# Products with a zero operand in a two-layer decode kernel, and new orders of the engines' work

## The chip, the cores and the metric

The kernel runs on one core of a Trainium2 chip. The core has a matrix engine (TensorE, PE in the profile, with its weight loads as PEld), three vector-like engines (VectorE or DVE, ScalarE or ACT, GpSimd or POOL), a queue engine (SyncE or SP) that here only issues DMAs, and sixteen DMA engines between HBM and the on-chip memory SBUF. Matrix products are written to PSUM, eight banks of 128 partitions by 512 fp32 columns. Each engine works through its own list of instructions in order and waits on semaphores for the others. The metric is the time on the device in microseconds (us): the median of several executions, less is better.

## The reference

Eight tokens (one per sequence of the batch, D = 448) go through two layers, which use the same weights and the same caches. Each layer is an attention block and an MLP block, with a residual around each:

```python
W = min(4096, max(256, Sk // 4))            # 1024 of 4096 cached positions
q = x @ wq                                   # 16 heads of 256
k, v = last W positions of the caches        # 8 heads, each used by two of q's
p = softmax(q . k * Dh ** -0.5); o = p . v
A(x) = o @ wo
B(x) = silu(x @ w1) @ w2                     # F = 1792

x = x + A(layernorm(x)); x = x + B(layernorm(x))
x = x + A(layernorm(x)); x = x + B(layernorm(x))
```

Everything is bf16 in memory. The window of the caches is 64 tiles of K and 64 of V (8 rows of the batch by 8 heads), 512 KB each, 67 MB; the weights are about 10.5 MB.

## The kernel before

**Rows.** The kernel goes through the batch row by row (b = 0 to 7). The K and V tiles of a row (sixteen, 8.4 MB) are loaded once and serve both layers, so all of a row's work of layer 1 and its attention of layer 2 happens while they are on the chip. A tile lies in one of 30 slots. The loads are issued by SP in one fixed sequence (K of row 0, `wo`, `w2`, V of row 0, `w1`, K of row 1, and so on), and the load that reuses a slot waits until the last reader of the tile in it is done: K loads of row b+2 wait for layer-2 scores of row b, V loads mostly for its layer-2 values.

**Steps of a row**, by the names that the program gives them:

- `KT`: DVE transposes each K tile in two halves (L629).
- `qbd1` (POOL, L619) spreads the queries of layer 1; `S0` (PE, L644) are the layer-1 scores, in two halves `S0.0`, `S0.1` of four groups of eight products each; `max0`, `mT0`, `mg0`, `mb0` (DVE, L657 to L661) find the maxima; `exp0` (ACT, L663); `perm0` (PE, L665) and `turn0` (DVE, L667) bring the weights p into columns; `l0` sums them.
- `PVA`, `PVD` (PE, L708, L727): values of heads 0 to 3 and 4 to 7. `oevA`, `oevD` (ACT, L697, L702) copy them out, `oTA`, `oTD` (PE, L688) turn them, `oTevA`, `oTevD` (DVE, L682) scale them.
- `woA`, `woD` (PE, L780), `rowb1` (ACT copy, L1054), `fold1` (PE, L498 and L500): output projection, added to x in bank 7.
- The chain between the attentions: `xb1` (DVE, L806), `stat1` (PE, L813), `var1` and `pow1` (the layernorm's scale, ACT L816 and POOL L818), `w1` (PE, L515), `yT` (DVE, L535), `tanh` (ACT, L825), `hT` (DVE, L826), `w2` (PE, L837), `rowb2` (ACT, L841), `fold2`, `xb2`, `stat2`, `var2`, `pow2`, and the queries of layer 2: `wq0`, `wq1` (PE, L864), `qT`, `qm` (DVE, L873), `qd` (PE, L877), `qbd2` (ACT, L881).
- `S1.0`, `S1.1`, `max1`, `exp1`, `perm1`, `turn1`, `l1`, `lc1` (ACT copy of the sums, L673): scores of layer 2, in bank 1 (`SC[1]`). `PV1.0`, `PV1.1` (PE): its values; `oev1`, `oT1`, `oTc1` (ACT, L679) store them for the end.

The layer-1 attention of row b+1 runs beside the chain and the layer-2 attention of row b. The output projection and MLP of layer 2 are done once for rows 0 to 6 (`final_rows`, names ending in 8, row 6.5) during the last row, and then for row 7 (`final_last`, names ending in L).

`stat1` and `oT1` share a bank, and so do other steps; two accesses to one bank from different engines are ordered by semaphores. The start-up work of row 0 also includes sums over the weights' rows (`rsum`, L434 on DVE and L442 on ACT, then `rsumd`), which the projections need for the layernorm's mean.

**What sets the order.** The program adds steps as tasks, one after the other, with the tiles that they read and write. Four strings (`ORDER`) then say for each engine in which order its tasks are emitted: each character is the place, in the list of tasks still left, of the one that comes next. Waits follow from the tiles, whatever the order. Where the text says that a step stands ahead of another, this order is meant. For a row from the middle of the program PE's order before is:

```text
fold1/4 oT1/3 stat1/4 w1/4 S0.0/5 S0.0/5 w2/4 S0.0/5 fold2/4 S0.0/5 wq0/4 stat2/4 wq1/4 qd0/4
S1.0/4 x4  S0.1/5 x4  qd1/4  S1.1/4 x4  perm0/5 l0/5  PVA/5 x4  perm1/4 ...
```

(name/row; x4 are four groups of products).

Of the kernel before, what the change touches and what calls it, by code (L numbers as in the profile page):

```python
# [14 lines left out]

ORDER = {
    "pe": (
        "0000000111110000022222102220100000077066000001111777700000223333200099227011440302200000706605100011"
        "1177770000022333320009222055510020111000070666010001111777700000244440220092222504444100110000706050"
        "0001111177770000024444012009222204440020111000077060510001111777700000223333011092222044410201110000"  # L20
        "70660510001111777700000223333011092222044441001110000777001400cc0bb0000000002233330110bb209110055020"
        "222000009991070550002010333333331011d00000222201000000000"),
    "dve": (
        "CnEDDoo.18B.17AiE.13y2xmd2odEUUErbixAlOzpyA1qNLyttwwhhBrh7yge0dakv0jo2nkici908gf4e4dn772kaaaa4h94215"
        "89940736350dccc03aaaa3321eb0c09b0088700555504000100a90888807700daa0bc0807700555504000000a90888077700"
        "da09a0a087700555504000000a90888077700da0bb00a77700555550000000a90888077700daa0aa0a08700555504000000a"
        "09888078700daa0990a07700555504000000a0898807870b0aba09aa90000555504000000b0ja0088e8d9998000504440300"
        "100001111100000000"),
    "act": (
        "1333342344233413d3c342322252222221111113122222010000000020111111110000002011111100000000201111111000"  # L30
        "00002011100000000000201111111100000020111100000004030200010010000000"),
    "pool": (
        "00010011022002200220022002200320001000"),
}


# [164 lines left out]
def bass_interleave_layers__sliding_block_cached__dense_activation_silu__decode_kernel(  # L201
# [3 lines left out]
    _, HKV, SK, DH = A_k_cache.shape  # L205
# [5 lines left out]
    P = 128  # L211
# [24 lines left out]
    ident = sb("ident", [P, P], BF16)  # L236
# [12 lines left out]
    cols = sb("cols", [P, 10], BF16)  # L249
# [51 lines left out]
    def pe(fns, reads, writes, row, name):  # L301
        add("pe", fns, reads=reads, writes=writes, row=row, name=name)
# [518 lines left out]
    def up(b, name):  # L821
# [4 lines left out]
        dve(lambda e: e.scalar_tensor_tensor(out=hTr[b], in0=th, scalar=1.0, in1=y, op0=ALU.add, op1=ALU.mult),  # L826
            bk(XB) + ["th"], ["hT"], b, "hT" + name)

    def chain(b):
        xcols(b, "1")  # L830
        stats(b, "1")
        up(b, "")
        if b < LAST:
            fns = []
            for f in range(FC):
# [3 lines left out]
                    stop=(f >= FC - 4), tile_position=(0, 32 * (f % 4)), skip_group_check=True))  # L839
# [3 lines left out]
        else:  # L843
            WB = (XB, LB[1])
            for part in range(2):
                fns = []
                for f in range(FC):
# [3 lines left out]
                        start=(f < 4), stop=(f >= FC - 4), tile_position=(0, 32 * (f % 4)), skip_group_check=True))  # L851
# [10 lines left out]
        for k2 in range(2):  # L862
# [4 lines left out]
                start=(c == 0 and s == 0), stop=(c == KC - 1 and s == 1), tile_position=(0, 32 * j), skip_group_check=True)  # L867
# [101 lines left out]
    def final_last(s):  # L969
        b = LAST  # L970
        scr = slots[s][:, :]
        KEY = SL(s)
        xr = scr[:, 0:XC + 1]
        orow = scr[:, 128:128 + 112]
        xrow_f = scr[:, 512:512 + 224].bitcast(F32)
        xs = view(bank[YB][:], 0, [(XS, XC + 1)])
        pe(lambda e: e.matmul(xs, ident[:], x2b[b], start=True, stop=True),
           ["ident", ("x2b", b)], bk(YB), b, "xinitL")
        for i0 in range(0, NCH, 16):
            wo_rows(b, range(i0, i0 + 16), lambda i: oT2[b][:, i % 2, i // 2:i // 2 + 1],  # L980
                    [("oT2", b, i0 // 16)], "woL")
        act(lambda e: e.activation(rowb, bank[XB][:, 0:D + 2], ACTF.Copy), bk(XB), [("rowb", 0), ("rowb", 1)], b, "rowbL")
        fold(b, ["rowb_e", ("rowb", 0), ("rowb", 1)], "L")
        xcols(b, "L")
        act(lambda e: e.activation(xr, bank[YB][:, 0:(XC + 1) * XS:XS], ACTF.Copy), bk(YB), ["xr"] + KEY, b, "xr")
        stats(b, "L")
        up(b, "L")
        ob = bank[OB[0]]
        T = 112
        fns = []  # L990
        for t in range(4):
            for c in range(KC):
                d0, d1 = max(T * t, P * c), min(T * t + T, P * c + P, D)
# [14 lines left out]
        pe(fns, ["hT"] + W2_R, bk(OB[0]), b, "w2L")  # L1008
        dve(lambda e: e.scalar_tensor_tensor(out=orow, in0=ob[:, 0:T], scalar=rhalf, in1=xrow_f, op0=ALU.mult,
                                             op1=ALU.add), bk(OB[0]) + KEY + ["xrowf", "rhalf"], ["orowL"], b, "orowL")  # L1010
        src = bass.AP(orow.tensor, orow.offset, [[32 * orow.ap[0][0], 4], [1, T]])
        dma(lambda e: e.dma_start(out2[b:b + 1].rearrange("o (t n) -> (o t) n", t=4), src), ["out_last"], "out",
            reads=["orowL"])
# [107 lines left out]
```

## Time and profile before

| | us |
|---|---|
| median of 3 runs | 245.74 |
| lowest, highest | 244.15, 248.39 |
| the profiled execution | 246.33 |
| its span, first to last instruction | 244.3 |
| PE busy | 166.2 (68%) |
| DVE busy | 154.6 (63%) |
| ACT busy | 69.5 (28%) |
| POOL busy | 22.8 (9%) |
| mean granted TensorE clock | 0.964 |

The page is of one execution. Its slices divide the span into 40 parts of 6.1 us; a digit is the busy share in tenths. PEclk is the share of full speed that the clock of TensorE was granted. "Chain" is the work that ended last, followed back from the end: what each step waited for. Rows of groups give the line of the code, the engine, the tiles and their shapes, how many there were, the time that they were busy and the mean time of one in ns, then idle time of the engine just ahead of them and what ended it. The span leaves out what lies around the program: 246.33 against 244.3.

### The profile page before, as it was taken

The page shows a single profiled execution, that of the slowest core. Times are in us where ns is not written, and L with a number is a line of the kernel's source. Part 1 is how long each engine was busy: PE and PEld are TensorE (multiplying, and loading weights), DVE is VectorE, ACT ScalarE, POOL GpSimd, SP SyncE. Part 2 cuts the span into 40 slices and gives each one's busy share as a digit, 9 for nine tenths or more (in the row PEclk, how much of TensorE's full clock was granted, in tenths as well). Part 3 has the DMA queues.
Part 4 walks back from the last instruction along what each step waited for, and adds up shares of the span by engine and source line. Part 5 has one row for each costly group of instructions (what it writes and reads, how often), then busy time and mean ns, then how long its engine had stood idle before and what let it go on. Part 6 is the DMA issues. An engine that isn't in the chain of part 4 may idle for free.

```text
span 244.3 us, 7993 instructions
## 1 busy us (share of the span) xinstructions
PE 166.2 (68%) x3521; PEld 93.1 (38%) x3521; DVE 154.6 (63%) x412; ACT 69.5 (28%) x205; POOL 22.8 (9%) x42
## 2 busy tenths in 40 slices
PE   0000516376879587978787887779779787998872
PEld 0000503023553345445444434443454444356532
DVE  2019897999774685668477758945864983165501
ACT  2000004991223522331332223233223322233230
POOL 1000030002001100100011002001000200011100
PEclk9999999999999899979999999999999998599996
DMA  6999999999989997999999999989999998000000
GB/s 158 401 406 404 380 380 406 407 408 411 404 294 372 415 406 253 388 413 373 331 412 409 379 385 412 408 298 406 412 365 369 413 406 302 3 3 3 3 4 1
DMA packets 23400, 78.18 MB, mean 320 GB/s; under 512 B 3127, under 2 KB 6086, under 8 KB 22982
## 3 DMA queue, kind: packets, MB, share of 16 engines
q1 hardware_dynamic: 22806, 77.30, 81.8%
q8 instruction: 27, 0.44, 0.7%
q10 hardware_dynamic: 560, 0.38, 0.7%
q14 instruction: 7, 0.06, 0.1%
HBM read 77.67 MB, written 0.01 MB: 318 GB/s over the span
## 4 chain that ended last, share of the span: by engine, by line
PE 42%; DVE 25%; DMA 14%; ACT 8%; issue 5%; SPq 3%; POOL 2%; DVEq 0%; ACTq 0%
DMA slot<-in_A_k_cache_dram 14%; PE bank L644 11%; DVE slot L629 9%; PE bank L708 6%; PE bank L780 5%; PE bank L864 5%; PE bank L837 3%; DVE slot L434 3%; SPq L455 2%; PE bank L877 2%; PE bank L727 2%; PE bank L515 2%; ACT rowb L841 2%; PE bank L498 2%; DVE bank L535 1%
## 5 line engine op out<-in xcount | busy, mean ns | idle before, releaser
L629 DVE STREAM_TRANSPOSE slot<-slot 128x512 uint32<-128x512 uint32 x128 | 82.3, 683 | 17.4 <-DMA slot<-in_A_k_cache_dram 17.2
L644 PE MATMUL bank<-slot,qbd 128*16 128x256 bf16 (+1 forms) x1024 | 40.7, 292 | 10.9 <-ACT qbd L881 5.2
L708 PE MATMUL bank<-slot,qbd 128*4 128x512 bf16 (+1 forms) x384 | 29.4, 406 | 7.5 <-DVE qbd L667 4.0
L644 PEld LDWEIGHTS bank<-slot,qbd 128*16 128x16 bf16 (+1 forms) x1024 | 25.3, 90 | 21.2 <-ACT qbd L881 7.5
L818 POOL TENSOR_TENSOR fcols<-fcols 128x1 f32<-128x1 f32 x17 | 9.5, 557 | 110.3 <-ACT fcols L816 107.8
L780 PE MATMUL bank<-wo_sb,q1s 128*1 128x449 bf16 x284 | 18.1, 386 | 1.6 <-DVE q1s L682 1.0
L864 PE MATMUL bank<-wq_sb,xbz 128*2 128x256 bf16 x512 | 17.0, 275 | 0.9 <-DVE xbz L806 0.7
L619 POOL TENSOR_TENSOR qbd<-q1s,fcols 128x256 bf16<-128x256 bf16 x16 | 9.5, 612 | 73.9 <-PE bank L688 70.3
L657 DVE TENSOR_REDUCE mm<-bank 128x1 f32<-128x256 f32 x16 | 6.8, 422 | 13.6 <-PE bank L644 13.6
L881 ACT ACTIVATE qbd<-bank 128x256 bf16<-128x256 f32 x16 | 6.1, 383 | 30.6 <-PE bank L877 30.6
L708 PEld LDWEIGHTS bank<-slot,qbd 128*4 128x4 bf16 (+1 forms) x384 | 7.9, 85 | 15.9 <-issue 5.8
L667 DVE STREAM_TRANSPOSE qbd<-bank 128x256 bf16<-128x256 bf16 x16 | 7.4, 463 | 10.1 <-PE bank L772 5.1
L548 PE MATMUL bank<-xb,cols 128*128 128x8 bf16 x4 | 0.3, 174 | 19.9 <-DVE slot L546 19.9
L535 DVE STREAM_TRANSPOSE bank<-bank 128x256 f32<-128x256 f32 (+1 forms) x25 | 10.9, 434 | 4.4 <-PE bank L515 1.5
L663 ACT ACTIVATE qbd<-bank,mm 128x256 bf16<-128x256 f32 x16 | 7.6, 472 | 18.6 <-DVE mm L661 13.8
L864 PEld LDWEIGHTS bank<-wq_sb,xbz 128*2 128x2 bf16 x512 | 11.2, 82 | 4.0 <-DVE xbz L806 1.7
L682 DVE TENSOR_TENSOR q1s<-bank,q1s 128x16 bf16<-128x16 f32 (+1 forms) x18 | 3.0, 168 | 14.2 <-PE bank L688 14.1
L702 ACT ACTIVATE qbd<-bank 128x512 bf16<-128x512 f32 x14 | 8.3, 595 | 10.2 <-PE bank L688 5.7
L697 ACT ACTIVATE qbd<-bank 128x256 bf16<-128x256 f32 x22 | 8.3, 382 | 9.5 <-PE bank L708 3.2
L806 DVE SCALAR_TENSOR_TENSOR xbz<-bank,fcols 128x5 bf16<-128x5 f32 x17 | 3.9, 227 | 10.7 <-PE bank L500 9.4
L727 PE MATMUL bank<-slot,qbd 128*12 128x512 bf16 (+3 forms) x124 | 10.4, 434 | 0.1
L837 PE MATMUL bank<-w_sb,q1s 128*1 128x449 bf16 x98 | 8.3, 434 | 3.1 <-DVE q1s L826 2.9
(156 smaller groups left out, 220.9 us busy)
## 6 DMA issues: line engine op xcount, KB each, us to landing
slot<-in_A_k_cache_dram SPq DMA_DIRECT2D x64, 512.0 KB, 8.5
slot<-in_A_v_cache_dram SPq DMA_DIRECT2D x64, 512.0 KB, 10.5
wo_sb<-in_A_wo_dram SPq DMA_DIRECT2D x1, 3584.0 KB, 25.9
wq_sb<-in_A_wq_dram SPq DMA_DIRECT2D x3, 1024.0 KB, 9.1
w_sb<-in_B_w_dram SPq DMA_DIRECT2D x1, 1568.0 KB, 28.1
w_sb<-in_B_w_dram SPq DMA_DIRECT2D x1, 1344.0 KB, 17.8
wq_sb<-in_A_wq_dram SPq DMA_DIRECT2D x1, 256.0 KB, 3.6
wq_sb<-in_A_wq_dram ACTq DMA_DIRECT2D x1, 256.0 KB, 4.4
```

Of the source, the lines that this page charges most:

```text
L535: dve(lambda e: e.transpose(view(bank[bi][:], n, [(2, n // 32), (n // 16, 16), (1, 2)]), bank[bi][:, 0:n].rearrange("p (g r s) -> p g r s" ...
L619: pool(lambda e, k2=k2: e.tensor_tensor(qdata(0, k2), q1s[:, b, 64 * k2:64 * k2 + 64].rearrange("p (n r) -> p n r", r=2).unsqueeze(3) .bro ...
L629: dve(lambda e, v=v: e.transpose(v, v), SL(s, h), SL(s, h), b, "KT%d" % k)
L644: fns.append(lambda e, w=w, j=j, kv=kv, cb=cb, par=par: e.matmul(sc[32 * j:32 * j + up_to, 0:256], w, kv, start=(cb == 0 and par == 0), st ...
L697: act(lambda e, s=s: e.activation(E_sb[L], ob[:, s * DH:(s + 1) * DH], ACTF.Copy), bk(OB[L]), QB(L, 1), b, "oev%s.%d" % (name, s))
L702: act(lambda e: e.activation(full, ob[:, :], ACTF.Copy), bk(OB[L]), QB(L, 0) + QB(L, 1), b, "oev" + name)
L708: return [lambda e, u=u: e.matmul(bank[OB[L] if ob is None else ob][32 * j:32 * j + 2 * n, :], pT_sb[L][:, pcol(u, c0):pcol(u, c0) + 2 * n ...
L727: pe([lambda e, t=t, c0=c0, w=w, kvh=kvh: e.matmul(bank[OB[0]][32 * t:32 * t + 2 * w, :], pT_sb[0][:, pcol(2 * t, c0):pcol(2 * t, c0) + 2 ...
L780: fns.append(lambda e, i=i, w=w, c0=c0: e.matmul(bank[XB][32 * (i % 4):32 * (i % 4) + 1, c0:c0 + D + 1], oT(i), w, start=(i < 4), stop=(i ...
L818: pool(lambda e: e.tensor_tensor(rhalf, var4, nhalf, ALU.pow), ["var4", "nhalf"], ["rhalf"], b, "pow" + name)
L837: fns.append(lambda e, f=f, w=w, c0=c0: e.matmul(bank[XB][32 * (f % 4):32 * (f % 4) + 1, c0:c0 + D + 1], hTr[b][:, f:f + 1], w, start=(f < 4),
L864: pe([lambda e, j=j, c=c, s=s, wb=wb, k2=k2: e.matmul(bank[wb][32 * j:32 * j + 2, 0:256], pair(b, xcol(c, k2), s), view(wq_sb[:], c * HD + ...
```

## The change

A function `busy(b, n)` adds n tasks on PE. Each is one product of a column of zeros, taken as 128 equal weight columns, with the identity read four times over (512 columns). Its result, zeros, goes over the whole of bank 1, which holds the layer-2 scores later in the row. As it writes that bank, it waits for the bank's readers in the row before. `chain` calls it with 8 in row 0 and 5 in the others, `final_last` with 5: 50 products in all.

All four order strings are new. Read out, PE's order for the row above becomes:

```text
fold1/4 oT1/3 zero/4 stat1/4 w1/4 zero/4 zero/4 zero/4 w2/4 S0.0/5 S0.0/5 fold2/4 S0.0/5 stat2/4 wq0/4 wq1/4
qd0/4 zero/4 S0.0/5  S1.0/4 x4  S0.1/5 x4  qd1/4  S1.1/4 x2  perm0/5  S1.1/4 x2  PVA/5 x4  l0/5 oTA.0/5 ...
```

In the other middle rows the last zero product stands behind `fold2` and the first mostly ahead of `oT1`. On DVE `turn0` moves ahead of `max1`, both halves of a K tile's transposes mostly follow each other, and one half stands between `yT` and `hT`; `oTevD` of rows 1, 2 and 4 moves ahead of the next row's transposes. On ACT `oevA.0` moves ahead of `exp1`, `lc1` ahead of `rowb1` (that of row 5 behind it), and a load of the activation table (the task `init` of L327) moves from row 1, between `oev1` and `oTc1`, to row 5, between `lc1` and `rowb1`. On POOL one of the two `qbd1` moves behind `pow2` from row 4 on. In the start-up many of DVE's small tasks move ahead of the first K tile, and the sums over weights stand elsewhere.

```diff
@@ ORDER
-    "pe": (
-        "0000000111110000022222102220100000077066000001111777700000223333200099227011440302200000706605100011"
...
+    "pe": (
+        "000000011111l111133312223022051002010033300710500300111117777000440033333210011004403330201101044000"
...
@@ up
+    def busy(b, n, row=None):
+
+        for _ in range(n):
+            pe(lambda e: e.matmul(bank[SC[1]][:, :], cols[:, 3:4].broadcast_to([P, P]), view(ident[:], 0, [(0, 4), (1, P)]),
+                                  start=True, stop=True), ["cols0", "ident"], bk(SC[1]), b, "zero")
+
     def chain(b):
+        busy(b, 8 if b == 0 else 5)
         xcols(b, "1")
         stats(b, "1")
         up(b, "")
@@ final_last
         dve(lambda e: e.scalar_tensor_tensor(out=orow, in0=ob[:, 0:T], scalar=rhalf, in1=xrow_f, op0=ALU.mult,
                                              op1=ALU.add), bk(OB[0]) + KEY + ["xrowf", "rhalf"], ["orowL"], b, "orowL")
+        busy(b, 5)
         src = bass.AP(orow.tensor, orow.offset, [[32 * orow.ap[0][0], 4], [1, T]])
```

More of the change, by code (lines that the diff above doesn't have):

```diff
@@ L17 @@
     "pe": (
-        "0000000111110000022222102220100000077066000001111777700000223333200099227011440302200000706605100011"
[L19 to L22, printed above, removed]
@@ L23 @@
-    "dve": (
[L24 to L28, printed above, removed]
+        "000000011111l111133312223022051002010033300710500300111117777000440033333210011004403330201101044000"
@@ new lines @@
+        "1770000300111117777000400444423010011155510022011101044000177005000011111777700040044442320001115514"
+        "0022201101044000177710000011111777700040044442320001161514002201110004400017716111101111177770004004"
+        "4442320001161510022201110105400017771000001111177770004004444232000116151002201111010033001777710100"
+        "ccc0b1111060000444442200011817771002022220000033ccc43a02060500001140333333300110000022220b1200000000"
+        "11000"),
+    "dve": (
+        "pSG0G0bGq0njnwvZtutFtUEg4CQz0g4yBydzjhvHwbvnFrEAAzkayz352iuj9k6q935nikb8g14f2a4439nj90888c8685c09664"
+        "4551122baaa2a929216bd1aaa10077700555555000010098880870705ac09a90087700555550000100098880870705ac09aa"
+        "0077700555550000100a08880878060aab09a0087700555550000100098880870705aa0aa90077700555550000100a088808"
+        "78060aab0990087700555550000100098880778060acb0b99a900005555500000000099ag90ebb8ba8006004403020100001"
+        "111100000000"),
@@ L29 @@
     "act": (
-        "1333342344233413d3c342322252222221111113122222010000000020111111110000002011111100000000201111111000"
-        "00002011100000000000201111111100000020111100000004030200010010000000"),
+        "13333442444455f5e56432322224222111111113312211111111111331211111111111133122111111111113312211111111"
+        "11133122100000000000220111000000000302011000000004002200010010000000"),
     "pool": (
-        "00010011022002200220022002200320001000"),
+        "00010011022002200200020002000010001000"),
```

## The prediction

> **What bounds the kernel now.** I read the page first: its slices, then its chain.
>
> ```profile
> PEclk9999999999999899979999999999999998599996
> DMA  6999999999989997999999999989999998000000
> GB/s 158 401 406 404 380 380 406 407 408 411 404 294 372 415 406 253 388 413 373 331 412 409 379 385 412 408 298 406 412 365 369 413 406 302 3 3 3 3 4 1
> PE 42%; DVE 25%; DMA 14%; ACT 8%; issue 5%; SPq 3%; POOL 2%; DVEq 0%; ACTq 0%
> DMA packets 23400, 78.18 MB, mean 320 GB/s; under 512 B 3127, under 2 KB 6086, under 8 KB 22982
> ```
>
> The DMA row says "always busy" for 34 slices (up to about 207 us), then nothing for 37 us. But the rate row has holes (294, 253, 331, 298, 365). At the 410 GB/s of the good slices 78.18 MB take 191 us; with some 4 us of start the stream could end near 195. So about 11 us are lost in holes, and the chain is mostly PE and DVE: the loads wait for slots that the compute frees late. The DMA queue's own waits agree.
>
> ```profile
> SPq L455 <- PE bank L644: 66.4, 7, 12.2
> ```
>
> The queue that issues K and V loads waits seven times for the score products (L644): a row's layer-2 scores free the slots of the row after next. So the time from one row to the next is compute, and the stream follows. I cut the trace by stretches at the starts of `rowb1` (L1054), once per row:
>
> ```profile
> 80.02:103.19 23.17, 17.93 (x380) 10.24 (x382) 15.24 (x38) 7.46 (x19) 2.21 (x4) 0.93 0.95 362
> 103.19:126.00 22.81, 18.76 (x396) 10.54 (x388) 15.55 (x39) 6.29 (x19) 2.37 (x5) 0.93 0.97 379
> 126.00:147.81 21.81, 17.16 (x388) 9.55 (x382) 15.13 (x37) 6.06 (x18) 2.21 (x4) 1.00 1.01 395
> 147.81:169.31 21.50, 17.40 (x392) 9.56 (x387) 14.60 (x37) 6.36 (x19) 2.37 (x5) 1.00 0.98 377
> 169.31:190.71 21.40, 17.54 (x391) 9.85 (x387) 15.16 (x38) 6.21 (x17) 2.29 (x4) 1.00 0.99 386
> 190.71:215.33 24.62, 20.35 (x400) 10.64 (x396) 14.32 (x38) 6.53 (x21) 1.10 (x2) 0.86 0.66 256
> ```
>
> Columns are the stretch, its length, then busy us of PE, weight loads, DVE, ACT, POOL, then clock, DMA share, GB/s. Rows with clock 1.00 take 21.4 to 21.8 us; the three with a lower clock take 22.8, 23.2 and 24.6. No engine is full (PE 17 to 18 of 21.5 us): a row is a string of waits between engines. The clock itself, stretch by stretch (PE alone):
>
> ```profile
> 83.30:86.70 3.40, 2.71 (x50) 0.50 1.05 414
> 107.20:110.60 3.40, 3.22 (x45) 0.50 1.03 406
> 206.10:213.00 6.90, 6.67 (x61) 0.51 0.18 67
> 240.30:244.30 4.00, 0.61 (x32) 0.50 0.01 2
> ```
>
> Half clock in four stretches, each a multiple of 3.4 us. The stretch of 3.4 us before each fall, and one before which nothing fell:
>
> ```profile
> 79.86:83.27 3.41, 1.26 (x37) 0.96 (x36) 2.94 (x6) 2.85 (x6) 0.00 (x0) 1.00 1.02 417
> 103.75:107.16 3.41, 2.14 (x59) 1.33 (x55) 2.67 (x7) 1.40 (x5) 0.55 (x1) 1.00 1.03 417
> 202.74:206.15 3.41, 1.66 (x42) 1.11 (x31) 0.87 (x3) 0.45 (x2) 0.00 (x0) 1.00 0.75 263
> 236.87:240.28 3.41, 1.99 (x90) 1.71 (x94) 0.83 (x3) 0.86 (x4) 0.55 (x1) 1.00 0.00 0
> 172.01:175.43 3.42, 2.23 (x57) 1.04 (x46) 3.00 (x7) 0.91 (x2) 0.41 (x1) 1.00 1.03 411
> ```
>
> PE was busy 37%, 63%, 49% and 58% of the stretch before a fall, and 65% of one that had none. The line lies near 64%: one product more in a stretch can decide.
>
> **The change part by part.** *The products.* Reading the new PE order out: in rows 1 to 6 mostly one zero product after `fold1`, three between `w1` and `w2`, one after `fold2`; eight in row 0; in the last row five in the chain and five in the final part: 50 in all. Whole-array products of 512 columns have no row in this trace; the nearest are these.
>
> ```profile
> 143.68 1.04 PE L727 MATMUL bank<-slot,qbd 128*16 128x512 bf16 x16
> 149.75 0.24 PE L813 MATMUL bank<-xbz 128*128 128x1 bf16 x4 [0.38 <-DVE slot L629]
> 149.92 0.95 PE L515 MATMUL bank<-w_sb,xbz 128*2 128x224 bf16 x32
> 152.00 0.92 PE L837 MATMUL bank<-w_sb,q1s 128*1 128x449 bf16 x14 [0.50 <-DVE q1s L826]
> 173.46 0.17 DVE L826 SCALAR_TENSOR_TENSOR q1s<-th,bank 128x14 bf16<-128x14 f32 x1 [0.42 <-ACT th L825]
> ```
>
> Sixteen 512-column products, four side by side, take 1.04 us: 0.26 us per set of 512 columns, which I take (from nothing, where it fills a wait, to the double at half clock). So 50 cost 13 us of PE time. But `w1` ends at 150.87 and `w2` starts at 152.00: 1.13 us of waiting for DVE, ACT, DVE, in which three products (0.78 us) fit. Ahead of `stat1` PE idles 0.38 us, so one fits; behind `fold2` I take the same. Today score products of the next row (L644) fill the `w1` gap; the new order moves them behind `w2`, where PE waits for ACT's copy `rowb2`, and behind `qd0`, where it waits for ACT. Cost: 0. A product also waits for readers of its bank; the last, `lc1` on ACT, is moved ahead of `rowb1` in nearly all rows, so it is done by then. If that cover is gone, the 13 us appear.
>
> *What the products give.* In the chain, the same stages at half and full clock:
>
> ```profile
> 70.47 7.13 DMA slot<-in_A_k_cache_dram
> 77.62 1.30 DVE slot L629 x2
> 81.08 1.28 ACT L327
> 82.95 1.29 PE bank L515 x32
> 85.34 1.49 PE bank L837 x8
> 107.38 1.50 PE bank L837 x10
> 119.44 1.06 PE bank L708 x16
> 149.99 0.91 PE bank L515 x21
> 152.00 0.86 PE bank L837 x12
> 203.78 1.15 issue
> 206.20 1.91 PE bank L708 x13
> ```
>
> Row 1: `w1` 1.29 against 0.91, `w2` 1.49 against 0.86: −1.0. Row 2: 0.64 in `w2`, some more in the scores behind it; −1.0 agrees with its 22.81 against 21.6. Last row: the first product of values takes 1.91 where 1.06 is usual (−0.85); the 6.67 us of PE work at half clock would be 3.3 less at full; not all of it is on the path, so −2.8. The fall at 240.3 comes after a 3.4 us stretch whose late part alone gets two products: 0. Together −4.8; bounds 0 and −6.3 (half of 2.71, 3.22 and 6.67).
>
> *The issue gap.* At 203.78 PE stood 1.15 us inside one group of scores with no cause shown, and this made the third fall. Other code lies there now, but such a gap can come elsewhere: −0.6, between 0 and −1.15.
>
> *ACT's table load.* It is moved from row 1, where it holds 1.28 us of the chain between `oev1` and `oTc1` (which `stat1` waits for), to row 5 ahead of `rowb1`.
>
> ```profile
> 167.00 0.18 ACT L673 ACTIVATE q1s<-bank 128x16 f32<-128x16 f32 x1
> 169.31 0.55 ACT L1054 ACTIVATE rowb<-bank 128x450 bf16<-128x450 f32 x1 [2.13 <-PE bank L780]
> ```
>
> There ACT idles 2.13 us, and 1.28 fits. `stat1` waits for `oTc1` without the load too (0.38 us in row 4, above), so 1.28 less 0.38: −0.9, between 0 and −1.28.
>
> *DVE in row 1.* `oTevD` stood behind two K transposes of row 2, which waited for the 7.13 us load above; it now stands ahead of them. But `xb1` still stands behind four. Between 0 and the 1.30 us of the two; I take −0.4.
>
> *Steady rows.* `perm0` moves into the middle of `S1.1`, and `turn0` ahead of `max1`; the exponential it needs is ready no sooner than today, so nothing. Half a K tile's transpose (0.65 us, half of the 1.30) now stands between `yT` and `hT`; DVE idles 0.42 there today, so +0.2 a row. `stat2` moves ahead of `wq0`, so that its power is ready earlier; I take 0.2 a row back for it. Sum 0, bounds ±0.3 in six rows, ±1.8.
>
> *Start.* This row sum of three weight chunks stands on the chain ahead of `turn0` of row 0:
>
> ```profile
> 43.25 2.80 DVE slot L434
> ```
>
> In its place comes one of two chunks, two thirds or 1.9 us by the same row; but two long sums now stand ahead of `max0`, and one more sum on ACT ahead of `exp0`. Half of the 0.9 arrives, −0.5; the bounds are half a sum either way, ±1.5.
>
> **Sum:** −4.8 −0.6 −0.9 −0.4 +0 −0.5 = −7.2. The profiled execution took 246.33 us, 2.03 around a span of 244.3; it lies 0.59 above the median of 245.74. So 246.33 − 7.2 = **239.1 us**, a span of 237.1.
>
> **The rivals.** *The products do not hold the clock*, or the new order opens other gaps: then −0.6, −0.9, −0.4, −0.5 stay: 243.9. For it: with zero weights nothing shows that the gate counts such products as work; one near-miss stretch per row at 65% leaves little margin. Against it: the fall went with PE's busy share in four of four. [...]
>
> *The stream swallows the early rows.* K loads land 7 us or more behind the scores that free their slots, and `xb1` stands behind four transposes of them; if that loop sets the pace, the 3.3 us of rows 1 and 2 (1.0 + 1.0 + 0.9 + 0.4) do not reach the end, nor does the start, and −2.8 and −0.6 stay: 242.9. For it: 70.47 on the chain. Against: 11 us of holes that shrink when slots come free earlier.
>
> *The products stand on the path.* Mechanism: PE works in order, so a product that starts just before its successor is ready holds it, and scores no longer in the `w1` gap lengthen what follows. All 50 exposed with no clock gained: 243.9 + 13 = 256.9; it is over 2% slower from about half exposed (6.8 of 13 us). For it: gaps of 0.3 to 0.4 us hold a 0.26 us product barely. Against: the 1.13 us gap takes three of five.
>
> *More.* With slots free earlier the holes close too: half of 11 us beside the last row's −2.8 and −0.6, and the rest: 246.33 − 5.5 − 3.4 − 1.8 = 235.6.
>
> **How the numbers follow.** Forecast 0.48; clock not held 0.21; stream swallows 0.12; on the path 0.12; more 0.07. Two per cent, about what a measurement of this kernel can tell from no change, are 240.8 and 250.7. Of the forecast's cases most lie under 240.8 (0.43 of 0.48), with *more* 0.50. The path rival gives slower 0.11 (a little of it stays within). The rest, 0.39, is within. Range: from 234.5, past *more*, to 249.0, past 243.9 with the unknowns of start and steady rows added (1.5 + 1.8) and a few products exposed.
>
> **What would show it.** Right: clock 1.00 in all stretches from row 1 to the last scores; row lengths of 21.4 to 21.8 throughout; no table load on the chain; `w1` 0.91 and `w2` 0.86 in rows 1 and 2; the zero products' PE time in stretches that were idle; `rowb1` of the last row near 208 instead of 215.33. Wrong: half-clock stretches as before; `w2` later than 1.15 us after `w1`; `stat1` waiting for the zero products; a gap in ACT's row 5 over 1.3 us; longer holes in the GB/s row.

## The result, and the profile after

The changed kernel takes 235.64 us (median of 4 runs, 235.11 to 237.31) beside 244.94 us for the kernel before (4 runs, 242.53 to 248.39): a ratio of 0.966, with a 95% interval of 0.957 to 0.976. Ratios here leave out runs more than 1.5% above the fastest of their kernel, in each later session more than half of those of the kernel before, so they can show less of a gain than the medians. The forecast of 239.1 us had the sign right, the main mechanism, and two thirds of the gain. The profiled execution took 235.61 us with a span of 233.7, against 246.33 and 244.3.

From the page of the kernel after: granted clock, DMA engines and rate in 40 slices of 5.8 us, then the DMA totals, the queue that brings instructions, the chain's shares, and the group of the zero products.

```profile
PEclk9999999999999999999999999999999999999999
DMA  6999999999999999999999999999999998300000
GB/s 163 413 403 407 379 381 399 407 407 412 405 403 392 414 404 356 365 414 409 400 406 406 400 400 409 409 326 407 410 406 382 411 409 329 127 3 3 3 1 4
DMA packets 23401, 78.20 MB, mean 335 GB/s; under 512 B 3127, under 2 KB 6086, under 8 KB 22982
q8 instruction: 28, 0.46, 0.8%
PE 47%; DVE 22%; DMA 13%; ACT 10%; issue 5%; SPq 2%; ACTq 0%; DVEq 0%
L833 PE MATMUL bank<-ident,cols 128*128 128x512 bf16 x48 | 16.2, 391 | 0.0
```

No slice behind the first record of the clock (at 54.1 us) is under full clock any more, and the holes in the rate row are fewer and shallower: 356, 365, 326 and 329 where there were 294, 253, 331 and 298. PE's share of the chain rose from 42% to 47%, DVE's fell from 25% to 22%. The zero products are 48 (8 in row 0, 5 in each of the seven other rows, 5 at the end), not the 50 that the description and the prediction count. They take 16.2 us, but PE as a whole is busy only 2.0 us longer than before (168.2 against 166.2). The same cut by rows as in the prediction, from one `rowb1` (now L1063) to the next, after; the columns are the stretch, its length, busy us of PE, weight loads, DVE, ACT and POOL, the clock, the DMA share and GB/s:

```profile
56.45:77.55 21.10, 17.69 (x385) 9.57 (x384) 15.07 (x39) 5.76 (x18) 3.36 (x6) 1.00 1.02 402
77.55:98.74 21.19, 17.98 (x391) 10.24 (x387) 15.37 (x38) 6.06 (x18) 2.37 (x5) 1.00 1.00 382
98.74:120.09 21.35, 18.61 (x401) 10.27 (x393) 16.01 (x40) 6.06 (x18) 1.72 (x3) 1.00 1.02 406
120.09:141.19 21.10, 18.14 (x393) 9.98 (x387) 14.63 (x38) 5.95 (x18) 2.30 (x4) 1.00 1.03 404
141.19:162.34 21.15, 18.55 (x395) 10.17 (x391) 15.80 (x39) 7.34 (x19) 2.30 (x4) 1.00 1.00 386
162.34:183.30 20.96, 18.15 (x393) 9.99 (x387) 14.51 (x37) 5.99 (x17) 1.68 (x3) 1.00 1.02 401
183.30:204.80 21.50, 18.01 (x403) 10.14 (x399) 15.23 (x41) 6.32 (x20) 2.27 (x4) 1.00 0.78 305
```

The clock is 1.00 in all seven and every row takes 21.0 to 21.5 us. Side by side, with what the prediction gave each stretch (row b begins at its own `rowb1`; its "last row" is row 6 here):

| stretch | before | after | change | forecast |
|---|---|---|---|---|
| start to `rowb1` of row 0 | 57.13 | 56.45 | -0.7 | -0.5 |
| row 0 | 22.90 | 21.10 | -1.8 | 0 |
| row 1 | 23.17 | 21.19 | -2.0 | -2.3 |
| row 2 | 22.81 | 21.35 | -1.5 | -1.0 |
| rows 3, 4, 5 | 64.72 | 63.21 | -1.5 | 0 |
| row 6 | 24.61 | 21.50 | -3.1 | -3.4 |
| from `rowb1` of row 7 to the end | 28.96 | 28.92 | 0 | 0 |
| sum | 244.3 | 233.7 | -10.6 | -7.2 |

The chain of waits of the kernel after, at `w1` (L516) and `w2` (L845) of rows 1 and 2:

```profile
79.52 0.90 PE bank L516 x32
...
81.56 0.91 PE bank L845 x10
...
100.92 0.91 PE bank L516 x29
...
102.97 0.91 PE bank L845 x12
```

Where row 1 had 1.29 and 1.49 us, both steps now take 0.9 us: full clock. The products of row 4 on PE's timeline (start, length, operation, idle time ahead):

```profile
142.61 0.38 PE L833 MATMUL bank<-ident,cols 128*128 128x512 bf16 x1
143.14 0.24 PE L814 MATMUL bank<-xbz 128*128 128x1 bf16 x4 [0.15 <-ACT q1s L680]
143.30 0.94 PE L516 MATMUL bank<-w_sb,xbz 128*2 128x224 bf16 x32
144.18 0.82 PE L833 MATMUL bank<-ident,cols 128*128 128x512 bf16 x3
145.42 0.92 PE L845 MATMUL bank<-w_sb,q1s 128*1 128x449 bf16 x14 [0.42 <-DVE q1s L827]
```

Three products take 0.82 us between `w1` and `w2`, and PE still waits 0.42 us for `hT` behind them. One fits ahead of `stat1`, which still waits 0.15 us for ACT. `w2` starts 1.18 us after `w1` ends; it was 1.13.

### The profile page after: what moved, and what is told of

It is laid out like the page before. It is cut to its first block, busy times and chain, and to the rows that moved or that the text cites. A ratio compares the mean times of both kernels' runs of the same rounds, so it can differ in the third digit from the quotient of the medians.

```text
span 233.7 us, 8070 instructions
## 1 busy us (share of the span) xinstructions
PE 168.2 (72%) x3569; PEld 93.4 (40%) x3569; DVE 155.3 (66%) x412; ACT 68.5 (29%) x205; POOL 22.8 (10%) x42
## 4 chain that ended last, share of the span: by engine, by line
PE 47%; DVE 22%; DMA 13%; ACT 10%; issue 5%; SPq 2%; ACTq 0%; DVEq 0%
DMA slot<-in_A_k_cache_dram 13%; PE bank L645 11%; DVE slot L630 9%; PE bank L709 7%; PE bank L872 6%; PE bank L781 4%; DVE slot L435 3%; PE bank L845 2%; ACT qbd L664 2%; PE bank L728 2%; PE bank L516 2%; ACT slot L443 2%; PE bank L885 2%; ACT qbd L698 1%; PE bank L666 1%
## 5 line engine op out<-in xcount | busy, mean ns | idle before, releaser
L645 PEld LDWEIGHTS bank<-slot,qbd 128*16 128x16 bf16 (+1 forms) x1024 | 23.9, 88 | 17.8 <-ACT qbd L889 7.2
L709 PE MATMUL bank<-slot,qbd 128*4 128x512 bf16 (+1 forms) x384 | 27.9, 388 | 1.8 <-DVE xb L584 1.3
L781 PE MATMUL bank<-wo_sb,q1s 128*1 128x449 bf16 x284 | 17.0, 362 | 0.4 <-ACT wo_sb L447 0.4
L833 PE MATMUL bank<-ident,cols 128*128 128x512 bf16 x48 | 16.2, 391 | 0.0
L728 PE MATMUL bank<-slot,qbd 128*12 128x512 bf16 (+3 forms) x124 | 11.2, 408 | 0.0
L443 ACT ACTIVATE slot<-w_sb 128x448 bf16<-128x448 bf16 x6 | 3.5, 576 | 22.3 <-DMA w_sb<-in_B_w_dram 22.2
L845 PE MATMUL bank<-w_sb,q1s 128*1 128x449 bf16 x98 | 6.5, 353 | 4.8 <-DVE q1s L827 4.8
```

Source lines behind the costliest of these rows:

```text
L645: fns.append(lambda e, w=w, j=j, kv=kv, cb=cb, par=par: e.matmul(sc[32 * j:32 * j + up_to, 0:256], w, kv, start=(cb == 0 and par == 0), st ...
L709: return [lambda e, u=u: e.matmul(bank[OB[L] if ob is None else ob][32 * j:32 * j + 2 * n, :], pT_sb[L][:, pcol(u, c0):pcol(u, c0) + 2 * n ...
L728: pe([lambda e, t=t, c0=c0, w=w, kvh=kvh: e.matmul(bank[OB[0]][32 * t:32 * t + 2 * w, :], pT_sb[0][:, pcol(2 * t, c0):pcol(2 * t, c0) + 2 ...
L781: fns.append(lambda e, i=i, w=w, c0=c0: e.matmul(bank[XB][32 * (i % 4):32 * (i % 4) + 1, c0:c0 + D + 1], oT(i), w, start=(i < 4), stop=(i ...
L833: pe(lambda e: e.matmul(bank[SC[1]][:, :], cols[:, 3:4].broadcast_to([P, P]), view(ident[:], 0, [(0, 4), (1, P)]), start=True, stop=True), ...
L845: fns.append(lambda e, f=f, w=w, c0=c0: e.matmul(bank[XB][32 * (f % 4):32 * (f % 4) + 1, c0:c0 + D + 1], hTr[b][:, f:f + 1], w, start=(f < 4),
```

## The experiments

All are timed against the kernel before, on the chip and in the session of each. Times that name rows come from each kernel's profiled execution.

### The parts alone

**e1_orders_only**: the new orders without the products.

```diff
     def busy(b, n, row=None):

-        for _ in range(n):
+        for _ in range(0):
```

> The changed kernel's four orders with all 50 products left out (the other steps in the same order). Theory (the products hold the clock, the orders give the smaller part): the clock falls again in some stretches between row 1 and the end and rises late in the start-up, so 240 to 242 us. Rival (the orders alone give the gain, the products ride along): 235 to 237 us with the clock at 1.00 or nearly, or with falls that cost nothing.

Measured: 242.23 us (241.18 to 243.81), ratio 0.988 (0.981 to 0.994). The rows take 24.53, 21.23, 22.07, 20.95, 21.12, 20.95 and 22.19 us. The long ones hold half-clock stretches (until 70.5 us in row 0, 108.0 to 111.4, 193.3 to 196.8), and the others are as short as those of the kernel after. PE in row 2, `w1` and `w2`:

```profile
105.69 0.94 PE L515 MATMUL bank<-w_sb,xbz 128*2 128x224 bf16 x32
107.81 1.50 PE L844 MATMUL bank<-w_sb,q1s 128*1 128x449 bf16 x14 [1.18 <-DVE q1s L826]
```

The orders move the score products out of the wait between `w1` and `w2`. Without the zero products PE stands still there for 1.17 to 1.63 us in every row, and the clock falls in some. The clock does not fall behind every such wait. The stretch of row 5 with the longest one, PE 52% busy (1.79 of 3.42), and the stretch behind it:

```profile
169.45:172.87 3.42, 1.79 (x60) 1.17 (x52) 3.29 (x8) 0.60 (x3) 0.55 (x1) 1.00 1.03 413
172.87:176.28 3.41, 2.70 (x87) 2.02 (x81) 2.63 (x6) 1.07 (x3) 1.02 (x2) 1.00 1.02 407
```

The orders do shorten the rows that keep their clock by about 0.5 us: the mean of rows 3 to 5 is 21.01 us here, 21.07 after, 21.57 before.

**e2_products_old_orders**: the products put into the orders of before (one behind `fold1`, three ahead of `w2`, one behind `fold2`, the start-up and the end as after). `lc1` moves ahead of `rowb1` on ACT, since otherwise ACT would wait for PE and PE, at the product behind `fold1`, for ACT.

```diff
+        busy(b, 8 if b == 0 else 5)
...
+        busy(b, 5)
...
-        "1333342344233413d3c342322252222221111113122222010000000020111111110000002011111100000000201111111000"
-        "00002011100000000000201111111100000020111100000004030200010010000000"),
+        "1333342344233413d3c342322252222221111113122211100000000020111000000000002011100000000000201110000000"
+        "00002011100000000000201110000000000020111100000004030200010010000000"),
```

> The 50 products in the old orders: put at the matching places (one behind fold1, three ahead of w2, one behind fold2; the extra ones of the first and last row as in the changed kernel), and ACT's lc1 moved ahead of rowb1, since a product waits for it. Theory (products hold the clock): clock 1.00 from the first rows on, 1.7 us from an earlier rise in row 0, 2.0 in rows 1 and 2, 2.8 in the last row: about 239 us. Rival (orders alone): 244 to 246 us.

Measured: 243.45 us (241.97 to 245.24), ratio 1.000 (0.994 to 1.006): no gain clear of the noise, though the median lies 1.9 us under that of before in its session (245.34). One half-clock stretch is left between the start-up and the end, 82.5 to 85.9 us in row 1, which takes 23.54 us. Ahead of it PE stands still 1.33 us ahead of `stat1`, because ACT loads its table there in the old order. Rows 3 to 5 take 21.98, 21.52 and 21.37 us, as in the kernel before, and a gap of 0.96 us without a cause stands at 202.17. So neither part has the gain alone.

### Is it the time that the products keep PE busy?

**e3_64_columns**: the same products in the same places, 64 columns instead of 512. The list of instructions is as long as that of the kernel after, instruction by instruction. (The "gate" of the expectation stands for what grants TensorE its clock.)

```diff
-            pe(lambda e: e.matmul(bank[SC[1]][:, :], cols[:, 3:4].broadcast_to([P, P]), view(ident[:], 0, [(0, 4), (1, P)]),
+            pe(lambda e: e.matmul(bank[SC[1]][:, 0:64], cols[:, 3:4].broadcast_to([P, P]), ident[:, 0:64],
```

> The changed kernel with products of 64 columns instead of 512, same count and places. Theory (the gate goes by PE's busy share, so the length of the products matters): a 64-column product adds little, the time lies near that of the orders without products, 239 to 242 us. Rival (any product at these places is enough): 235 to 237 us.

Measured: 242.50 us (240.72 to 243.79), ratio 0.990 (0.983 to 0.996), 6.9 us over the median of the kernel after. Its PE in row 2, then stretches of 3.4 us before and in two falls:

```profile
105.45 0.26 PE L833 MATMUL bank<-ident,cols 128*128 128x64 bf16 x3
106.70 1.66 PE L845 MATMUL bank<-w_sb,q1s 128*1 128x449 bf16 x14 [0.98 <-DVE q1s L827]
```

```profile
102.97:106.38 3.41, 2.04 (x55) 1.40 (x51) 2.88 (x7) 1.37 (x5) 0.55 (x1) 1.00 1.02 408
106.38:109.79 3.41, 3.09 (x46) 1.57 (x46) 2.27 (x7) 0.64 (x1) 0.00 (x0) 0.50 1.03 410
167.82:171.23 3.41, 1.57 (x49) 1.14 (x51) 3.22 (x8) 1.06 (x4) 0.55 (x1) 1.00 1.03 412
171.23:174.65 3.42, 3.18 (x46) 1.77 (x45) 1.96 (x5) 0.64 (x1) 0.00 (x0) 0.50 1.02 406
```

The short products leave 0.98 us of the wait empty, and the clock falls behind stretches with PE 60% and 46% busy (2.04 and 1.57 of 3.41). The two rows that hold these falls take 22.22 and 22.16 us, 0.9 and 1.2 more than after. The largest loss is row 0's: the clock rises for good only at 68.8 us, and the row takes 24.24 us, 3.1 more. Half a clock in one chain costs about 1 us. The four rows without a fall (21.20, 21.05, 21.17, 21.14) are those of the kernel after (21.19, 21.10, 21.15, 21.50) within 0.05 in three, and the fourth takes 21.08 in e9 below with long products: the length of a product costs nothing that shows where the clock is held anyway.

**e12_three_of_five**: in rows 1 to 6 512 columns only for the three between `w1` and `w2` (two of them in row 6), and 64 for the others; row 0 and the end keep theirs.

```diff
+NARROW = {1: [0, 4], 2: [0, 4], 3: [0, 4], 4: [0, 4], 5: [0, 4], 6: [0, 1, 4]}
...
+            w = 64 if i in NARROW.get(b, ()) else 512
```

> The changed kernel with only the products between w1 and w2 of rows 1 to 6 at 512 columns (three a row, two in row 6); the others of these rows have 64. Count and positions in the code unchanged. Theory (the 3.4 us stretches that fall are those with the wait between w1 and w2, which the three fill): 235 to 237 us, clock 1.00 in rows 1 to 6. Rival (all five are needed, since the stretches lie anywhere): falls in some rows, 237 to 241 us.

Measured: 235.91 us (235.39 to 237.02), ratio 0.959 (0.953 to 0.966), the clock full until 232.0 us. Three of five are enough; the one ahead of `stat1` and the one at `fold2` are not needed at full length.

**e4_doubled**: every product twice.

```diff
-            pe(lambda e: e.matmul(bank[SC[1]][:, :], cols[:, 3:4].broadcast_to([P, P]), view(ident[:], 0, [(0, 4), (1, P)]),
-                                  start=True, stop=True), ["cols0", "ident"], bk(SC[1]), b, "zero")
+            pe([lambda e: e.matmul(bank[SC[1]][:, :], cols[:, 3:4].broadcast_to([P, P]), view(ident[:], 0, [(0, 4), (1, P)]),
+                                   start=True, stop=True)] * 2, ["cols0", "ident"], bk(SC[1]), b, "zero")
```

> Every product issued twice, 100 in all, 13 us more of PE time. Theory (waits cover the 50, three of five in a gap of 1.13 us): the second set overruns the gaps, 0.3 to 0.8 us a row, 238 to 241 us. Rival (cover is large): 235 to 237 us. Rival (already the first set lies on the path): 13 us more, 248 us.

Measured: 242.88 us (240.85 to 243.64), ratio 0.988 (0.982 to 0.995), with a full clock from 57.3 us on. The rows take 21.63, 21.58, 21.62, 22.31, 22.68, 20.97 and 20.95 us. That is not an even price of five more products a row: rows 5 and 6 pay nothing, rows 0 to 2 pay 0.3 to 0.5 us, and rows 3 and 4 lose 1.2 and 1.5. PE in row 3:

```profile
135.87 0.27 PE L645 MATMUL bank<-slot,qbd 128*8 128x256 bf16 x1 [0.82 <-issue]
```

Two gaps of 0.82 and 1.00 us without a cause, like the one of before at 203.78, are most of what rows 3 and 4 lose. So this run does not give the price of an exposed product; it gave the question of where such gaps come from.

### The table load

**e5_table_row1**: the kernel after, with ACT's table load put back between `oev1` and `oTc1` of row 1; PE's list is unchanged.

```diff
-        "13333442444455f5e56432322224222111111113312211111111111331211111111111133122111111111113312211111111"
-        "11133122100000000000220111000000000302011000000004002200010010000000"),
+        "13333442444455f5e56432322224222111111113312211100000000022010000000000002201100000000000220110000000"
+        "00002201100000000000220111000000000302011000000004002200010010000000"),
```

> The changed kernel with ACT's table load put back to row 1, between oev1 and oTc1. Theory (its 1.28 us is on the path there and hidden in row 5): 0.9 us more, and one more if the 1.3 us of waiting on PE in front of stat1 makes the clock fall in row 1: 236.5 to 238 us. Rival (the move is worth nothing): 235 to 236 us.

Measured: 237.70 us (235.97 to 238.99), ratio 0.976 (0.966 to 0.986), by the medians 2.1 us over the kernel after; the intervals of the two ratios overlap, and the rows tell more. ACT in row 1 of this kernel, and the stretches of 3.4 us from there:

```profile
79.52 1.28 ACT L328 ACT_TABLE_LOAD   x1
80.81 0.20 ACT L680 ACTIVATE q1s<-bank 128x32 f32<-128x32 f32 x1
```

```profile
78.50:81.91 3.41, 1.85 (x49) 1.18 (x45) 2.64 (x6) 2.74 (x5) 0.19 (x2) 1.00 1.02 416
81.91:85.32 3.41, 3.41 (x39) 1.13 (x32) 2.77 (x6) 0.28 (x1) 0.41 (x1) 0.50 1.04 413
```

Row 1 takes 23.27 us instead of 21.19. The load holds `oTc1`, `stat1` waits, PE is 54% busy (1.85 of 3.41), and the clock falls although the zero products are there. In the kernel after the load stands in row 5's idle time of ACT:

```profile
160.56 1.28 ACT L328 ACT_TABLE_LOAD   x1
162.34 0.55 ACT L1063 ACTIVATE rowb<-bank 128x450 bf16<-128x450 f32 x1 [0.50 <-PE bank L781]
```

`rowb1` still waits 0.50 us for PE behind it: fully hidden.

### Where the instructions lie

The page's instruction queue brought 28 packets, 0.46 MB: 16 KB each. With 3569 products and as many weight loads for 28 packets, one holds some 255 instructions, about 128 products: an estimate that takes all 28 for PE's. It agrees with e9 below, which has 128 products and their loads more, and 29 packets. The gaps without a cause lie just behind such a packet: the one of before ends 1.25 us behind the end of one, at 204.93 us. So I moved the code of PE without touching its work: products of 16 columns at the very front of its list, into a bank that nothing else uses there, at a time when PE has nothing else to do.

```diff
+    for _ in range(40):
+        pe(lambda e: e.matmul(bank[YB][:, 496:512], cols[:, 3:4].broadcast_to([P, P]), ident[:, 0:16],
+                              start=True, stop=True, skip_group_check=True), ["cols0", "ident"], bk(YB), -1, "pad")
```

**e7_after_shift40**: the kernel after with these 40.

> The changed kernel with the same 40 products of 16 columns at the front of PE's list. Theory (where the fetches fall is part of its gain: it has no gap over 0.4 us of this kind): gaps of 0.5 to 1.2 us behind a fetch come up in some rows, 236 to 240 us. Rival (fetches play no part): 235 to 236.5 us, no such gap.

Measured: 244.93 us (243.92 to 245.37), ratio 1.006 (0.999 to 1.012). The whole gain is gone. The chain of this kernel, in the score products of rows 1, 2 and 3:

```profile
91.27 1.29 issue
...
113.81 1.36 issue
...
137.39 1.44 issue
```

The third of these on PE's timeline, and the instruction queue in the stretch from 136.4 to 137.6 us:

```profile
135.27 2.12 PE L645 MATMUL bank<-slot,qbd 128*16 128x256 bf16 x54
138.83 0.74 PE L645 MATMUL bank<-slot,qbd 128*8 128x256 bf16 x18 [1.44 <-issue]
```

```profile
q8 instruction: 1, 0.02, 5.6%
```

One packet, under way for 1.07 us (5.6% of 16 engines' 1.2 us): it begins at 136.47, when PE is in the middle of the scores, and ends at 137.54. PE runs dry at 137.39 and starts again 1.29 us after the packet's end. Four such gaps stand in this trace (1.29, 1.36, 1.44 and 1.60 us, in rows 1 to 4), each at a packet; a fifth of 1.44 us in row 0 stands at a packet too, but the profile puts its end down to ACT. They also make PE idle: behind the gaps in rows 2 and 3, right behind the same scores, the clock falls (117.4 to 120.9, 141.3 to 144.8), after stretches with PE 42% and 49% busy. Behind the one in row 1 it does not, after a stretch with 51% (1.74 of 3.41). Row 2 pays for a gap and a fall:

```profile
102.11:126.11 24.00, 20.13 (x401) 10.62 (x393) 16.00 (x40) 6.06 (x19) 1.72 (x3) 0.93 1.00 377
```

**e10_after_shift128**: 128 instead of 40, one packet's worth.

```diff
-    for _ in range(40):
+    for _ in range(128):
```

> The changed kernel with 128 products of 16 columns at the front of PE's list instead of 40. Theory (position of the code modulo 256 instructions decides): the changed kernel's time, 235 to 237 us, no gap over 0.5 us in rows 1 to 4. Rival (products at the front disturb something else): 243 to 245 us, as with 40.

Measured: 236.92 us (236.01 to 238.24), ratio 0.963 (0.956 to 0.971), no gap without a cause over 0.25 us in the scores, and row 2 is back:

```profile
99.96:121.56 21.60, 18.94 (x401) 10.39 (x393) 16.13 (x40) 6.07 (x19) 1.72 (x3) 1.00 1.02 396
```

More of the same padding restores the gain, so not the 40 products but the place at which PE's list is cut into packets made the loss.

**e6_before_shift40** and **e11_before_shift80**: the kernel before with 40 and with 80 of them.

> The kernel before with 40 products of 16 columns put at the very front of PE's list, where PE idles; nothing else moves, but each later instruction lies 80 or more places further in PE's code. In the trace of before an instruction fetch of 16 KB ran from 202.57 to 203.68 us and the gap of 1.15 us ended at 204.93, 1.25 behind its end; in the run with doubled products two such gaps ended 1.3 us behind a fetch. Theory (the gap is a fetch that falls into a dense stretch of scores, and it made the third fall of the clock): the gap is not at that place, the last row loses no 6.8 us at half clock, 241 to 243 us unless a gap comes elsewhere. Rival (the gap belongs to the place, not to the code's position): unchanged, 244 to 246 us, gap in S1 of row 6 again.

> The kernel before with 80 products of 16 columns at the front. With 40 it was no better (a gap of 0.88 us in row 6 again, one of 0.43 in row 3). Theory (the old orders lose to the new ones wherever the code is cut, since their waits let the clock fall anyway): 243 to 247 us whether or not a gap shows. Rival (the kernel before was merely cut badly): 238 to 241 us.

Measured: 246.80 us (244.97 to 248.39), ratio 1.014 (1.002 to 1.025), and 247.17 us (243.50 to 249.45), ratio 1.008 (1.000 to 1.015). With 40 the gap at 203.78 is gone, but one of 0.88 us comes at 208.21 and one of 0.43 in row 3, and the clock falls in rows 1, 2 and 3. Row 6, without a fall, takes 21.42 us instead of 24.61, but rows 0 and 3 take 24.43 and 24.68 instead of 22.90 and 21.82, so the time shows no gain. With 80 no such gap is left and row 6 takes 20.47 us, and the time is no better: the clock falls in rows 1 and 2 as before, and the start and row 5 are longer. At none of these three places of the cut is the kernel before near the kernel after, so it was not merely cut badly.

### A warm start

**e8_warm_start**: the kernel after with 40 more zero products of 512 columns in the idle time of the start-up (24 ahead of the first selection of queries, 4, 5, 4 and 3 later), to raise the clock earlier. **e9_warm_start_page**: the same, and 88 of the 16-column products at the front, so that 128 are added in all and the rest of the list is cut as in the kernel after.

```diff
+    for _ in range(40):
+        pe(lambda e: e.matmul(bank[OB[1]][:, :], cols[:, 3:4].broadcast_to([P, P]), view(ident[:], 0, [(0, 4), (1, P)]),
+                              start=True, stop=True), ["cols0", "ident"], bk(OB[1]), -1, "warm")
```

> The changed kernel with 40 more products in PE's idle times of the start-up (24 ahead of q1sel, 4 ahead of S0.0, 5 ahead of perm0, 4 ahead of PVA, 3 ahead of oTA.0, all of row 0, into another idle bank). In the changed kernel PE still works at half speed until some 54 us (16 value products take 1.9 us there where 1.03 is usual). Theory: the clock rises near 30 us and stays, row 0 gains 0.5 to 1.5 us: 234 to 235.2 us. Rival (the start is bound by ACT's and DVE's sums): 235 to 236 us, the clock up all the same.

> The changed kernel with the 40 start-up products of the run before (512 columns, in PE's idle times of row 0) and 88 products of 16 columns at the front: 128 products with their weight loads are 256 instructions, one fetch of 16 KB, so from row 1 on the code lies again as in the changed kernel. Theory (the 1.0 to 1.6 us gaps of the runs with 40 more products came from where the code was cut): no gap over 0.5 us, 234 to 236.5 us. Rival (more products as such cost it): 242 to 245 us as with 40.

Measured: 244.50 us (242.91 to 245.69), ratio 1.004 (0.995 to 1.014), and 236.06 us (235.57 to 237.87), ratio 0.962 (0.953 to 0.970). e8 has gaps of 1.05, 1.35 and 1.62 us in the scores of rows 1 to 3, the same loss as e7; e9 has none. The clock rises at 32.4 us in e9 (falling twice more before 57 us), and `rowb1` of row 0 starts at 57.19 us, no earlier than the 56.45 of the kernel after: an earlier rise of the clock does not shorten the start-up. No kernel here is clearly faster than the change itself.

## Why the prediction was right or wrong

**What bounds the kernel: right.** A string of waits between engines, with the loads following: the rows got shorter and the queue went along. SP's queue for K and V still waits mostly for score products (after; before it was 66.4 us in 7), and its waits sum to some 95 us in both traces:

```profile
SPq L456 <- PE bank L645: 70.0, 12, 11.1
```

**The products at no cost: right.** Not only in the wait between `w1` and `w2`: three of the four rows of e3 without a fall are no shorter with an eighth of the columns. (With 48 products the price of 13 us would be 12.5, and *on the path* 256.4; nothing else changes.) What a product costs where nothing covers it was not measured; e4 was meant for it and came out mixed with the gaps.

**What the products give (-4.8): right in mechanism, too small in reach, and in its places partly luck.** e3 changes nothing but the columns and loses 6.9 us by the medians, 5.8 by the ratios (0.990 less 0.966, of 245 us). Rows 1, 2 and 6 gave back 2.0, 1.5 and 3.1 us where the terms for them, with the gap, the table load and `oTevD`, made 2.3, 1.0 and 3.4. But of these three rows only row 2 falls in e3: rows 1 and 6 keep their clock with the short products too (21.20 and 21.14 us). What e3 loses lies in rows 0, 2 and 5 (3.1, 0.9 and 1.2 us). And row 6 is short in two kernels with the old orders and no zero products, e6 and e11 (21.42 and 20.47 us). So the -2.8 for row 6 came out, but that the products earned it is not shown; which rows fall differs from kernel to kernel. The term left out is row 0. In before PE was at half clock there, which the clock's records hide: they begin with the first rise, at 62.8 us, and the digits of the slices read 9 until then. (The last of the four stretches that the prediction lists, 4.00 us, is no multiple of 3.4: the span ends in it.) The lengths show it, `w1` of row 0 before and after:

```profile
58.61 1.66 PE L515 MATMUL bank<-w_sb,xbz 128*2 128x224 bf16 x32
```

```profile
57.89 0.95 PE L516 MATMUL bank<-w_sb,xbz 128*2 128x224 bf16 x32
```

After, the first rise is at 54.1 us, and row 0 lost 1.8 us. In the other kernels row 0 goes the same way: 24.24 and 24.53 us where the clock rises for good at 68.8 and 70.5 (e3, e1), and 21.11 and 21.63 where it does so at 56.7 and 57.3 (e10, e4).

**Zero weights as work: the first rival is refuted.** They count: e3 and e12 differ from the kernel after only in how long zeros are multiplied, and the clock follows: with all of them short it falls in three rows, with three of five long in none. The clock fell behind stretches of 3.41 us in which PE was 60% and 46% (e3) and 54% (e5) busy, with no gap in them over 1.52 us.

**The line near 64%: half right.** In the fourteen profiles no full-clock stretch of 3.4 us with PE over 64% busy comes before a fall. Of those inside the program with under 50%, all do. In between both occur: 60% fell in e3, 52% in e1 and 51% in e7 did not. So the share bounds the fall on two sides and does not decide it.

**The issue gap (-0.6): right by luck.** It went from 1.15 us to a largest of 0.36. I had taken half since "such a gap can come elsewhere", but bounded what it can do by that one gap. e7 shows what such gaps can do: four or five of them, with the falls that they cause, cost 9 us. The prediction had no case for it; had the change cut the list 40 products off, its 239.1 us would have failed for a reason that no row of before names except that 1.15 us.

**The table load (-0.9) and row 1's clock (-1.0): right as a sum, wrong as two terms.** e5 puts both back by the load alone: 2.1 us by the medians, and 2.1 us of row 1 in its profile. The load's wait is what let PE's share drop, so the products did not hold row 1 without the move; e2 shows the same, and e3 that without the load the short products were enough there. Its 1.28 us agree with what the traces had.

**`oTevD` (-0.4):** no run shows it alone; row 1 as a whole gave 0.3 less than its terms.

**Steady rows (0, bounds 0.3 a row): wrong.** The three rows at full clock in both kernels lost 0.7, 0.35 and 0.44 us, 0.5 on the mean. e1 has it without the products, so it comes from the orders. By the starts of the same steps in both traces it is spread out: in row 3 0.56 us between the two halves of `qbd2` (no change there in rows 4 and 5), and 0.34, 0.17 and 0.10 from `turn0` to the next `rowb1`; the rest is smaller moves, for and against. I had put `perm0` and `turn0` at nothing, "the exponential it needs is ready no sooner than today", and set 0.2 lost at the half transpose against 0.2 won at `stat2`. The sum of such small moves was not to be had from the rows that I read.

**Start (-0.5): came out**, -0.7, but not shown: e5, whose start-up is that of the kernel after, takes 57.37 us there, 0.9 more than the 56.45. **The final part: right**, 0.

**The other rivals.** The stream did not swallow rows 1 and 2. The products are not on the path. The time came out at *more* (235.6), but that it came by its mechanism, holes in the stream that close, is not shown. The start and the rows ahead of the last gave 7.5 us, and the holes in the rate shrank. What lies beyond the forecast is row 0 (1.8), which goes with its clock, and rows 3 to 5 (1.5), which go with the orders; the loads then start earlier and the holes follow. I had counted as gains only the rows in which the clock record showed a fall.

**What stays open.** Why PE runs dry at some packets among the dense short products, and not at the others, is not shown. The falls of before differ from run to run (its runs spread from 241.6 to 250.0 us over the sessions, with mean clocks from 0.907 to 0.989, those of the kernel after from 235.1 to 237.3); that the 3.4 us stretches begin elsewhere in each run would explain it, but is not shown. Within the trace of before the changes of the clock do lie on such a grid: from one to the next it is 20.5, 3.4, 20.5, 3.4, 95.5, 6.9 and 27.3 us, each a whole number of stretches of 3.41 within 0.1.

## What to carry to other kernels

Where PE waits about 1 us in every pass of a chain, look at its busy share over 3.4 us, the length of a half-clock stretch in these traces (3.41). In these runs no stretch over 64% busy came before a fall, every one under 50% inside the program did (37%, 42%, 46% and 49%), and between them it went either way (63%, 60%, 58% and 54% fell, 52% and 51% did not); a fall halved the clock for the next stretch (0.50) and cost about 1 us (0.9 and 1.2 in e3). Three products of 512 columns with a zero operand inside the wait held the clock here at no cost that showed (e12, 235.91 us beside 235.64), but not where another wait lay in the same stretch (e5, a table load of 1.28 us). When the code of an engine grows or shrinks, compare gaps without a cause in the dense stretches before judging the edit, and try it again with the list moved by a fraction of a packet. A clock row that begins with 9 may only mean that no record exists yet; the length of a known step tells (`w1` of row 0, 1.66 us before and 0.95 after).

## What the hardware showed that was not expected

The position of the code was worth as much as the change: 40 more tiny products ahead of everything cost 9.3 us (235.64 to 244.93), with 128 the medians differ by 1.3. All twelve gaps of PE of 0.8 us and more that the profiles of before, e2, e4, e6, e7 and e8 put down to nothing lie in score products, and end 1.25 to 1.54 us behind the end of a packet. The largest such gap at any other step in the fourteen profiles is 0.66 us (e8). The kernel after has 28 packets and no such gap over 0.36 us, but in the dense scores of e7 PE stands still for up to 1.60 us, and more is lost by the clock that falls behind the gaps in rows 2 and 3 (0.51 for 3.50 us each).
